# Sketch laid out by head, fewer warm-ups and earlier loads in the prologue of a fused attention and expert kernel

## The chip, the cores and the metric

The kernel runs on one core of one Trainium2 chip. The metric is device microseconds (us) of one execution; lower is better. All runs of one group are made on one chip, with runs of the kernel before between them.

Executions of this program fall into two groups that differ by a little over 1 us. They differ in the mean clock that TensorE was granted over the span. In the four timed groups the kernel before ran 44 times: 25 executions at a granted clock of 0.999 or 1.0 have a median of 500.97 us (499.89 to 501.62), 19 at 0.997 or less have 502.1 us (501.78 to 502.7). I call them full-clock and low-clock executions, and give full-clock medians where an effect is below 1 us. Some kernels have executions at 0.998; I count them as full-clock, since the one that was profiled (b_straight) has its only half-clock stretch of the trace's clock record after 498.15 us, behind the last matmul.

## The reference

```python
def phi(x):                                   # q, k, v: (4, 4, 1088, 32); S1, S2: (8, 32)
    a = np.einsum('rd,bhsd->bhsr', S1, x)
    b = np.einsum('rd,bhsd->bhsr', S2, x)
    return np.einsum('bhsi,bhsj->bhsij', a, b).reshape(*x.shape[:-1], r * r)
q_p, k_p = (phi(q), phi(k))
kv = np.einsum('bhsf,bhsd->bhfd', k_p, v)
z = np.sum(k_p, axis=2)
attn = num / (den + 1e-06)                    # num from kv, den from z
x = attn.transpose(0, 2, 1, 3).reshape(4352, 128)
p = domain_probs / (domain_probs.sum(-1, keepdims=True) + 1e-09)
for e in range(4):                            # w1: (4, 128, 1024), w2: (4, 1024, 128)
    h = np.maximum(x @ w1[e], 0.0)
    out += p[:, e:e + 1] * (h @ w2[e])
```

## The kernel before

The kernel is one long pipeline on TensorE. A prologue prepares the first 128 tokens: the sketch matrices S1 and S2 are converted from float64 bits, the keys of batch 0 are transposed (kT), projected (h), multiplied into features (kp), summed over all tokens (f, then kvz), and the first queries are attended (den, num, xT). After that, expert matmuls of 11 chunks of tokens run without a break, and the attention of later tokens is worked in between. The first and the last chunk (128 tokens) take plain matmuls; the middle ones use a scheme with seven products, for which GpSimd forms sums of the second layer's weights (w2s).

The loads, and the warm-up that raises TensorE's clock while they are under way:

```python
s_raw = cpool.tile([32, 2 * D], I32, name="s_raw")
nc.vector.memset(s_raw[:, :], 0)
for i, (eng, src) in enumerate(((nc.scalar, S1), (nc.sync, S2))):
    eng.dma_start(s_raw[R * i : R * i + R, :], src.bitcast(I32))
...
load_rows(k, 0, "kn")
load_rows(q, 0, "qn", slice(0, P))
...
nc.scalar.activation(idle[:, :], warm[:, 0:1], ACTF.Identity)
vn[0] = load_v(0, (nc.sync, nc.scalar))        # two value loads on the sync queue, two on scalar's
...
for i, t in enumerate((0, (B - 1) * S + G - 4)):
    nc.sync.dma_start(
        ends[:, i, :], bass.AP(domain_probs.tensor, domain_probs.offset + t * E, [[G * E, 32], [1, 4 * E]])
    )
load_rows(q, 0, "qn", slice(P, S))
for e in range(E):
    load_w1(e)
    load_w2(e)
...
for _ in range(14):
    wp = psum(ps_h, "h")
    nc.tensor.matmul(wp[:, :], warm[:, 0:P], warm[:, :], start=True, stop=True)
```

The end of a plain chunk, which is also the end of the program:

```python
if e == E - 1:
    t = (START[m] // S) * S + START[m] % S // 32
    nc.sync.dma_start(
        bass.AP(out.tensor, out.offset + t * DM, [[G * DM, 32], [1, 4 * DM]]), total.pop(m)[:, :]
    )
```

The loop hands out one weight sum after each step with `if i: next(to_sum, None)`.

## Time and profile before

| | value |
|---|---|
| time, first three runs | 500.92, 501.15, 500.92 us |
| span of the profiled execution (full clock) | 499.2 us |
| TensorE busy | 490.8 us, 98% |
| first key matmul / first expert matmul begins | 6.88 / 15.49 us |
| last operation on the result (`end`) begins | 495.75 us |

TensorE is busy for 98% of the span, so only three places are left to win at: the prologue before 15.49 us, the hole before "den" near 25 us, and what follows the last matmul. The third is in the timeline of the last microseconds, first VectorE's and then the sync queue's (columns: start, length, engine, line, operation, output<-input, idle time before it and its releaser):

```profile
core 0 of [0], span 499.2 us
...
495.75 0.35 DVE L657 SCALAR_TENSOR_TENSOR end<-o,ends,end 128x128 f32<-128x128 f32 x1 [0.76 <-PE o L186]
...
496.13 0.58 SPq L662 DMA_DIRECT2D out_dram<-end  x1
```

From the last vector operation to the end of the span there are 499.2 - 495.75 = 3.45 us: the operation, the issue of the store, its data, and its completion.

### The profile page before, as it was taken

The page shows a single profiled execution, that of the slowest core. Times are in us where ns is not written, and L with a number is a line of the kernel's source. Part 1 is how long each engine was busy: PE and PEld are TensorE (multiplying, and loading weights), DVE is VectorE, ACT ScalarE, POOL GpSimd, SP SyncE. Part 2 cuts the span into 40 slices and gives each one's busy share as a digit, 9 for nine tenths or more (in the row PEclk, how much of TensorE's full clock was granted, in tenths as well). Part 3 has the DMA queues.
Part 4 walks back from the last instruction along what each step waited for, and adds up shares of the span by engine and source line. Part 5 has one row for each costly group of instructions (what it writes and reads, how often), then busy time and mean ns, then how long its engine had stood idle before and what let it go on. Part 6 is the DMA issues. An engine that isn't in the chain of part 4 may idle for free.

```text
span 499.2 us, 11045 instructions
## 1 busy us (share of the span) xinstructions
PE 490.8 (98%) x4442; PEld 367.8 (74%) x4442; DVE 326.5 (65%) x749; ACT 250.7 (50%) x491; POOL 229.8 (46%) x264
## 2 busy tenths in 40 slices
PE   8899999999999999999999999999999999999997
PEld 6775788777776657777777777777777777788996
DVE  5858675868667585757657646558656557665643
ACT  4543553545454454544545455445455445556662
POOL 6730333444544263444545344344555355655571
PEclk9999999999999999999999999999999999999999
DMA  7981030021002330031001100021001100110000
GB/s 203 286 293 51 1 91 1 2 85 20 1 2 85 66 91 0 1 85 22 3 1 64 43 1 1 2 85 22 2 1 53 23 1 1 43 23 2 14 3 17
DMA packets 29666, 22.36 MB, mean 45 GB/s; under 512 B 20016, under 2 KB 26800, under 8 KB 29232
## 3 DMA queue, kind: packets, MB, share of 16 engines
q1 hardware_dynamic: 29312, 21.40, 15.3%
q8 instruction: 35, 0.57, 0.5%
q10 hardware_dynamic: 304, 0.26, 0.2%
q14 instruction: 15, 0.12, 0.1%
HBM read 19.35 MB, written 2.31 MB: 43 GB/s over the span
## 4 chain that ended last, share of the span: by engine, by line
PE 96%; DVE 3%; issue 0%; ACT 0%; DVEq 0%; ACTq 0%
PE h L186 48%; PE o L186 39%; PE f L186 5%; PE den L186 2%; PE num L186 1%; PE h L176 1%; DVE qp L420 1%; DVE hid L592 1%; DVE qa L479 0%; DVE qf L469 0%; DVE qb L474 0%; DVE qf L471 0%; DVE end L657 0%; ACT hid L618 0%; ACT fs L348 0%
## 5 line engine op out<-in xcount | busy, mean ns | idle before, releaser
L592 DVE SCALAR_TENSOR_TENSOR hid<-h,hid 128x256 f32<-128x256 f32 (+6 forms) x432 | 203.7, 472 | 149.0 <-ACT hid L618 140.7
L186 PE MATMUL h<-xT,w_sb 128*64 128x512 f32 (+4 forms) x1408 | 298.7, 496 | 1.7 <-DVE xT L454 1.4
L618 ACT ACTIVATE hid<-h 128x512 f32<-128x512 f32 (+3 forms) x288 | 158.3, 550 | 202.4 <-PE h L186 169.9
L186 PE MATMUL o<-hid,w2s 128*64 128x256 f32 (+3 forms) x1152 | 220.9, 355 | 0.0
L186 PEld LDWEIGHTS h<-xT,w_sb 128*64 128x64 f32 x1408 | 149.5, 137 | 52.7 <-issue 4.7
L186 PE MATMUL o<-hid,w_sb 128*64 128x256 f32 (+3 forms) x864 | 185.0, 356 | 0.6 <-DVE end L657 0.6
L186 PEld LDWEIGHTS o<-hid,w2s 128*64 128x64 f32 x1152 | 131.5, 137 | 31.7 <-issue 0.6
L733 POOL TENSOR_TENSOR ev<-yz,sh 64x256 f32<-64x256 f32 (+3 forms) x72 | 48.6, 675 | 159.0 <-ACT sh L736 156.3
L186 PEld LDWEIGHTS o<-hid,w_sb 128*64 128x64 f32 x864 | 101.4, 137 | 21.1 <-issue 1.6
L721 POOL TENSOR_TENSOR yz<-ev 128x512 f32<-128x512 f32 (+3 forms) x36 | 42.3, 1175 | 84.1 <-ACT ev L724 83.9
L733 POOL TENSOR_TENSOR ct<-ev 128x512 f32<-128x512 f32 (+3 forms) x36 | 42.2, 1173 | 2.8
L733 POOL TENSOR_TENSOR ct<-ct,gate 128x512 f32<-128x512 f32 (+3 forms) x27 | 31.9, 1183 | 2.1
L733 POOL TENSOR_TENSOR total<-total,ct 128x512 f32<-128x512 f32 (+3 forms) x27 | 31.8, 1177 | 2.1
L420 DVE TENSOR_TENSOR qp<-qa,qb 64x352 f32<-64x352 f32 (+2 forms) x44 | 31.6, 719 | 1.0
L610 ACT ACTIVATE hid<-h 128x256 f32<-128x256 f32 x24 | 15.3, 655 | 18.7 <-PE h L186 18.2
L723 ACT COPY ev<-o 128x512 f32<-128x512 f32 (+3 forms) x36 | 19.4, 538 | 9.4 <-PE o L186 8.9
L186 PE MATMUL o<-w_sb,hid 128*64 128x128 f32 x256 | 24.0, 273 | 0.0
L186 PEld LDWEIGHTS o<-w_sb,hid 128*64 128x64 f32 x256 | 19.9, 137 | 1.7 <-issue 1.5
L724 ACT COPY ev<-o 128x512 f32<-128x512 f32 (+3 forms) x36 | 19.4, 539 | 3.0
L359 DVE TENSOR_TENSOR kp<-fs 128x256 f32<-128x256 f32 (+1 forms) x24 | 16.1, 677 | 0.0
L736 ACT COPY sh<-yz 64x256 f32<-64x256 f32 (+3 forms) x36 | 13.7, 379 | 1.4 <-POOL yz L721 0.5
L737 ACT COPY sh<-yz 64x256 f32<-64x256 f32 (+3 forms) x36 | 13.7, 380 | 0.9
(93 smaller groups left out, 250.8 us busy)
## 6 DMA issues: line engine op xcount, KB each, us to landing
w_sb<-in_moe_w_dram SPq DMA_DIRECT2D x8, 512.0 KB, 7.7
gate<-gates SPq DMA_DIRECT2D x3, 1024.0 KB, 4.9
kn<-in_k_dram SPq DMA_DIRECT2D x4, 544.0 KB, 4.1
gate<-gates SPq DMA_DIRECT2D x2, 960.0 KB, 5.4
vn<-in_v_dram SPq DMA_DIRECT2D x14, 128.0 KB, 5.0
qn<-in_q_dram SPq DMA_DIRECT2D x3, 544.0 KB, 4.1
gate<-gates SPq DMA_DIRECT2D x1, 896.0 KB
out_dram<-ob SPq DMA_DIRECT2D x12, 64.0 KB, 2.0
```

Source lines behind the costliest of these rows:

```text
L186: nc.tensor.matmul(out(s), weights(s), moving(s), **flags)
L359: eng.tensor_tensor(out=_ap(kps[b], 0, P, 256 * t0 + P * p + 64 * x, [[256, n], [32, 2], [R, 4], [1, R]]), in0=in0, in1=_ap(fss[b], 0, P, ...
L420: nc.vector.tensor_tensor(out=qp[p][64 * x : 64 * x + 64, 0:n], in0=qa[64 * p : 64 * p + 64, 0:n], in1=qb[64 * p : 64 * p + 64, 0:n], op=A ...
L592: nc.vector.scalar_tensor_tensor(out=out, in0=src, scalar=0.0, in1=in1, op0=ALU.max, op1=ALU.subtract)
L610: nc.scalar.activation(turned, src, ACTF.Relu)
L618: nc.scalar.activation(hd[:, n * j : n * j + n], hp[:, 0:n], ACTF.Relu)
L721: add = lambda out, in0, in1, op=ALU.add: nc.gpsimd.tensor_tensor(out=out, in0=in0, in1=in1, op=op)
L723: nc.scalar.copy(_ap(ev, 0, P, 0, [[2 * w, 2], [1, w]]), _ap(a0, 0, P, 0, two))
L724: nc.scalar.copy(_ap(ev, 0, P, w, [[2 * w, 2], [1, w]]), _ap(a1, 0, P, 0, two))
L733: add = lambda out, in0, in1, op=ALU.add: nc.gpsimd.tensor_tensor(out=out, in0=in0, in1=in1, op=op)
L736: nc.scalar.copy(sh[HP:P, 0:w], yz[0:HP, 0, 0:w])
L737: nc.scalar.copy(sh[0:HP, 0:w], yz[HP:P, 1, 0:w])
```

## The change

The intent is a shorter prologue and a smoother start of the second chunk. The sketch matrix sk is laid out by head, so that four copies fill it instead of eight. The loads no longer wait for a memset, and the value loads go ahead of the scalar engine's dummy activation. Three sets of first factors of the queries replace four (12 matmuls instead of 16; the profile counts each as two). Eleven warm-ups replace fourteen. The rectified values of the plain chunks are written straight instead of turned, which needs the two `ends` loads and the store of the plain chunks in another order of tokens. The weight sums are handed out in the second half of the first chunk.

```diff
-    s_raw = cpool.tile([32, 2 * D], I32, name="s_raw")
-    nc.vector.memset(s_raw[:, :], 0)
+    s_raw = cpool.tile([R2, 2 * D], I32, name="s_raw")
...
     load_rows(q, 0, "qn", slice(0, P))
+    vn[0] = load_v(0, (nc.sync, nc.scalar))
...
     nc.scalar.activation(idle[:, :], warm[:, 0:1], ACTF.Identity)
-    vn[0] = load_v(0, (nc.sync, nc.scalar))
...
-            ends[:, i, :], bass.AP(domain_probs.tensor, domain_probs.offset + t * E, [[G * E, 32], [1, 4 * E]])
+            ends[:, i, :], bass.AP(domain_probs.tensor, domain_probs.offset + t * E, [[E, 4], [G * E, 32], [1, E]])
...
-    for _ in range(14):
+    for _ in range(11):
...
     for h in range(H):
-        nc.scalar.copy(
-            _ap(sk, 32 * h, 32, R2 * (h // 2) + 4 * (h % 2), [[H * R2, 2], [R, 2], [1, 4]]),
-            _ap(s_T, 0, 32, 0, [[D, 2], [4, 2], [1, 4]]),
-        )
-        nc.scalar.copy(
-            _ap(sk, 32 * h, 32, H * R + R * h, [[H * R2, 2], [1, R]]), _ap(s_T, 0, 32, R, [[D, 2], [1, R]])
-        )
+        nc.scalar.copy(_ap(sk, 32 * h, 32, R2 * h, [[HP, 2], [1, R2]]), _ap(s_T, 0, 32, 0, [[D, 2], [1, R2]]))
... (GpSimd's copies sp and sr: three sets instead of four)
... (key_project and key_product: the same matmuls and products in the layout by head)
-        fq = [psum(ps_o, "o0"), psum(ps_o, "o1")]
-        for i in range(2):
-            for p in range(2):
-                for j in range(2):
-                    both(fq[i][:, n * p : n * p + n], sr[:, 2 * i + p, j, :], qT[:, 0:n], start=(j == 0), stop=(j == 1))
+        fq = [psum(ps_o, "o0"), psum(ps_o, "o1"), psum(ps_n, "num")]
+        for i in range(3):
+            for j in range(2):
+                both(fq[i][:, 0:n], sr[:, i, j, :], qT[:, 0:n], start=(j == 0), stop=(j == 1))
...
-            src = _ap(hp, 0, P, 0, [[n, 2], [32, n // 32], [1, 32]])
-            turned = _ap(hd, 0, P, 0, [[n, 2], [1, n // 32], [n // 32, 32]])
...
-                nc.scalar.activation(turned, src, ACTF.Relu)
+                nc.scalar.activation(hd[:, 0 : 2 * n], hp[:, 0 : 2 * n], ACTF.Relu)
...
-                        bass.AP(out.tensor, out.offset + t * DM, [[G * DM, 32], [1, 4 * DM]]), total.pop(m)[:, :]
+                        bass.AP(out.tensor, out.offset + t * DM, [[DM, 4], [G * DM, 32], [1, DM]]), total.pop(m)[:, :]
...
-            if i:
+            if i > NQ // 2:
                 next(to_sum, None)
```

More of the change, by code (lines that the diff above doesn't have):

```diff
@@ L154 @@
         load_w2(e)
-    own2 = cpool.tile([P, 2], F32, name="own2")
     sk = cpool.tile([P, P], F32, name="sk")
-    sp = cpool.tile([32, 4, HP], F32, name="sp")
-    sr = cpool.tile([P, 4, 2, P], F32, name="sr")
+    sp = cpool.tile([32, 3, 2, 32], F32, name="sp")
+    sr = cpool.tile([P, 3, 2, P], F32, name="sr")
     sq = cpool.tile([P, P], F32, name="sq")
@@ L163 @@
     nc.gpsimd.memset(sq[:, :], 0.0)
-    nc.gpsimd.memset(own2[:, :], 0.0)
-    for h in range(H):
-        nc.gpsimd.memset(own2[32 * h : 32 * h + 32, h % 2 : h % 2 + 1], 1.0)
     kT = cpool.tile([P, P * NT], F32, name="kT")
@@ L171 @@
     nc.gpsimd.memset(vx[64:P, NT - 1, :, 0:D], 0.0)
-    for _ in range(14):
+    own2 = cpool.tile([P, 2], F32, name="own2")
+    nc.gpsimd.memset(own2[:, :], 0.0)
+    for h in range(H):
+        nc.gpsimd.memset(own2[32 * h : 32 * h + 32, h % 2 : h % 2 + 1], 1.0)
+    for _ in range(11):
         wp = psum(ps_h, "h")
@@ L194, in word @@
     def word(name, t=I32):
-        return cpool.tile([32, 2 * D], t, name=f"s_{name}")
+        return cpool.tile([R2, 2 * D], t, name=f"s_{name}")
     def bits(out, in0, s1, op0, s2=None, op1=ALU.bypass):
@@ L201, in either @@
         nc.vector.tensor_tensor(out=out, in0=a, in1=b, op=ALU.bitwise_or)
-    low = _ap(s_raw, 0, 32, 0, [[2, D]])
-    high = _ap(s_raw, 0, 32, 1, [[2, D]])
+    low = _ap(s_raw, 0, R2, 0, [[2, D]])
+    high = _ap(s_raw, 0, R2, 1, [[2, D]])
     hi, lo = slice(0, D), slice(D, 2 * D)
@@ L207 @@
     s_e, s_f, s_m, s_x, s_n = (word(n) for n in ("e", "f", "m", "x", "n"))
-    s_hl, s_T = word("hl", F32), word("T", F32)
+    s_hl = cpool.tile([32, 2 * D], F32, name="s_hl")
+    s_T = cpool.tile([32, 2 * D], F32, name="s_T")
+    nc.vector.memset(s_hl[:, :], 0.0)
     bits(s_f[:, hi], high, 1, shl, 21, shr)
@@ L222 @@
     either(s_f[:, :], s_e[:, :], s_m[:, :])
-    nc.vector.tensor_tensor(out=s_hl[:, :], in0=s_n[:, :], in1=s_f[:, :].bitcast(F32), op=ALU.mult)
+    nc.vector.tensor_tensor(out=s_hl[0:R2, :], in0=s_n[:, :], in1=s_f[:, :].bitcast(F32), op=ALU.mult)
     nc.vector.transpose(s_T[:, :], s_hl[:, :])
     for h in range(H):
-        nc.scalar.copy(
-            _ap(sk, 32 * h, 32, R2 * (h // 2) + 4 * (h % 2), [[H * R2, 2], [R, 2], [1, 4]]),
-            _ap(s_T, 0, 32, 0, [[D, 2], [4, 2], [1, 4]]),
-        )
-        nc.scalar.copy(
-            _ap(sk, 32 * h, 32, H * R + R * h, [[H * R2, 2], [1, R]]), _ap(s_T, 0, 32, R, [[D, 2], [1, R]])
-        )
-    for i in range(2):
-        for j in range(2):
-            nc.gpsimd.tensor_copy(
-                _ap(sp, 0, 32, HP * (2 * i + j), [[32, 2], [R, 4], [1, R]]),
-                _ap(s_T, 0, 32, D * j, [[4, 2], [1, 4], [0, R]]) if i else _ap(s_T, 0, 32, D * j + R, [[0, 2], [0, 4], [1, R]]),
-            )
-    for h in range(H):
-        for i in range(2):
-            nc.gpsimd.tensor_copy(
-                _ap(sr, 32 * h, 32, P * (4 * i + 2 * (h // 2)) + 32 * (h % 2), [[P, 2], [HP, 2], [1, 32]]),
-                _ap(sp, 0, 32, P * i, [[HP, 2], [32, 2], [1, 32]]),
-            )
+        nc.scalar.copy(_ap(sk, 32 * h, 32, R2 * h, [[HP, 2], [1, R2]]), _ap(s_T, 0, 32, 0, [[D, 2], [1, R2]]))
+    for i in range(3):
+        nc.gpsimd.tensor_copy(
+            _ap(sp, 0, 32, HP * i, [[32, 2], [R, 4], [1, R]]),
+            _ap(s_T, 0, 32, 4 * (i - 1) if i else R, [[D, 2]] + ([[1, 4], [0, R]] if i else [[0, 4], [1, R]])),
+        )
+    for h in range(H):
+        nc.gpsimd.tensor_copy(
+            _ap(sr, 32 * h, 32, 32 * h, [[P, 6], [1, 32]]), _ap(sp, 0, 32, 0, [[32, 6], [1, 32]])
+        )
     mask_lo = [R2 + l % R2 for l in range(32)]
@@ L336, in key_project @@
         if gi == 0:
-            fss[b] = apool.tile([P, 4, NT, R2], F32, tag="fs", name="fs")
+            fss[b] = apool.tile([P, 2, NT, 32], F32, tag="fs", name="fs")
             kps[b] = apool.tile([P, NT, 2, P], F32, tag="kp", name="kp")
@@ L340, in key_project @@
             for i in range(2):
-                both(
-                    kf[:, HP * t : HP * t + HP],
-                    kT[:, P * (t0 + t) : P * (t0 + t + 1)],
-                    sk[:, HP * i : HP * i + HP],
-                    start=(i == 0),
-                    stop=(i == 1),
-                )
+                for _ in range(2):
+                    on_side(
+                        lambda s: _ap(kf, HP * s, HP, 32 * t, [[P, 2], [1, 32]]),
+                        lambda s: kT[:, P * (t0 + t) + HP * s : P * (t0 + t) + HP * s + HP],
+                        lambda s: sk[:, HP * i : HP * i + HP],
+                        start=(i == 0),
+                        stop=(i == 1),
+                    )
         nc.scalar.copy(
-            _ap(fss[b], 0, P, R2 * t0, [[R2, n], [R2 * NT, 4], [1, R2]]),
-            _ap(kf, 0, P, 0, [[HP, n], [R2, 4], [1, R2]]),
+            _ap(fss[b], 0, P, 32 * t0, [[32 * NT, 2], [1, 32 * n]]), _ap(kf, 0, P, 0, [[P, 2], [1, 32 * n]])
         )
     def key_product(b, t0, n, p, x, eng, kf=None):
-        if kf is None:
-            in0 = _ap(fss[b], 0, P, R2 * (NT * p + t0) + R * x, [[R2, n], [4, 2], [1, 4], [0, R]])
-        else:
-            in0 = _ap(kf, 0, P, R2 * p + R * x, [[HP, n], [4, 2], [1, 4], [0, R]])
+        src, off = (kf, P * p) if kf is not None else (fss[b], 32 * (NT * p + t0))
         eng.tensor_tensor(
             out=_ap(kps[b], 0, P, 256 * t0 + P * p + 64 * x, [[256, n], [32, 2], [R, 4], [1, R]]),
-            in0=in0,
-            in1=_ap(fss[b], 0, P, R2 * (NT * (2 + p) + t0), [[R2, n], [R, 2], [0, 4], [1, R]]),
+            in0=_ap(src, 0, P, off + 4 * x, [[32, n], [R2, 2], [1, 4], [0, R]]),
+            in1=_ap(fss[b], 0, P, 32 * (NT * p + t0) + R, [[32, n], [R2, 2], [0, 4], [1, R]]),
             op=ALU.mult,
@@ L521, in start @@
             pass
-        fq = [psum(ps_o, "o0"), psum(ps_o, "o1")]
-        for i in range(2):
-            for p in range(2):
-                for j in range(2):
-                    both(fq[i][:, n * p : n * p + n], sr[:, 2 * i + p, j, :], qT[:, 0:n], start=(j == 0), stop=(j == 1))
+        fq = [psum(ps_o, "o0"), psum(ps_o, "o1"), psum(ps_n, "num")]
+        for i in range(3):
+            for j in range(2):
+                both(fq[i][:, 0:n], sr[:, i, j, :], qT[:, 0:n], start=(j == 0), stop=(j == 1))
         qb = apool.tile([P, QW], F32, tag="qb", name="qb")
-        nc.scalar.copy(qb[:, 0 : 2 * n], fq[0][:, 0 : 2 * n])
+        nc.scalar.copy(qb[:, 0:n], fq[0][:, 0:n])
         for x in range(2):
@@ L543, in start @@
         qp = query_tiles()
-        for p in range(2):
-            nc.vector.tensor_tensor(
-                out=qp[p][:, 0:n], in0=fq[1][:, n * p : n * p + n], in1=qb[:, n * p : n * p + n], op=ALU.mult
-            )
+        for x in range(2):
+            for p in range(2):
+                query_product(qp, p, x, n, fq[1 + x], qb)
         key_divide(b, kv)
@@ L603, in first @@
                 )
-            src = _ap(hp, 0, P, 0, [[n, 2], [32, n // 32], [1, 32]])
-            turned = _ap(hd, 0, P, 0, [[n, 2], [1, n // 32], [n // 32, 32]])
             if m and kq % 2:
-                nc.vector.tensor_scalar(out=turned, in0=src, scalar1=0.0, scalar2=None, op0=ALU.max)
+                nc.vector.tensor_scalar(
+                    out=hd[:, 0 : 2 * n], in0=hp[:, 0 : 2 * n], scalar1=0.0, scalar2=None, op0=ALU.max
+                )
             else:
-                nc.scalar.activation(turned, src, ACTF.Relu)
+                nc.scalar.activation(hd[:, 0 : 2 * n], hp[:, 0 : 2 * n], ACTF.Relu)
             work()
```

## The prediction

> **What bounds the kernel now.** I read the page's busy shares first, then the chain that ended last, then the timeline of the first 30 us and of the last 8 us, and last the order of instructions on each engine in both kernels. The busy shares say that TensorE is the bound, so only time in which TensorE waits, or works on something that the change removes, can be won.
>
> ```profile
> PE 490.8 (98%) x4442; PEld 367.8 (74%) x4442; DVE 326.5 (65%) x749; ACT 250.7 (50%) x491; POOL 229.8 (46%) x264
> ```
>
> The span is 499.2 us, so TensorE is not busy in 8.4 us. A table of busy time by stretch puts 1.25 us of that in the first 12 us, 1.85 us at 12 to 16 us, 0.5 us at 20 to 30, 0.9 us at 30 to 60, and some 3.5 us after the last matmul. From 60 to 480 us it is 0.5 us. "Busy" hides one more loss: warm-up matmuls count as busy. The chain of the first 16 us shows it (start, length, what):
>
> ```profile
> 0.81 0.11 DVE s_raw L118
> 0.92 0.28 DVE warm L135
> 1.25 5.63 PE h L176 x14
> 6.88 2.25 PE h L186 x72
> 9.13 1.75 PE o L186 x32
> 10.88 2.15 PE f L186 x72
> 13.12 0.30 DVE kvz L382
> 13.47 0.46 PE den L186 x4
> 13.96 0.33 DVE dT L442
> ```
>
> Fourteen warm-up matmuls hold TensorE until 6.88; then come key projections, query factors (o), key sums (f), and a chain across VectorE until the first expert matmul at 15.49. Everything before 15.49 is a prologue that shifts the whole rest. What else could have let the keys start earlier is in the timeline (start, length, engine, line, what; the bracket is idle time and its releaser):
>
> ```profile
> 0.95 0.41 SPq L120 DMA_DIRECT2D s_raw<-in_S_dram  x1
> 1.41 0.37 SPq L93 DMA_DIRECT2D kn<-in_k_dram  x1
> ...
> 2.76 0.17 DVE L198 TENSOR_SCALAR s_f<-s_raw 32x32 int32<-32x32 int32 x1 [1.56 <-DMA s_raw<-in_S_dram]
> ...
> 5.25 1.30 DVE L318 STREAM_TRANSPOSE kT<-kn 128x512 f32<-128x512 f32 x2 [0.52 <-DMA kn<-in_k_dram]
> ...
> 5.90 0.20 ACT L235 COPY sk<-s_T 32x16 f32<-32x16 f32 x1
> ```
>
> The first half of kT is done at 5.25 + 0.65 = 5.90, the eighth copy into sk at 6.10. So the inputs of the first key matmul were there at 6.10 and TensorE came at 6.88.
>
> **What the Trainium skill says.** "TensorE: Matmul & The Clock Gate", What's actually happening: the array starts at half clock and is released by some 3.4 us of sustained work, by time and not by number of matmuls, with a free-running window. The trace agrees in kind: the warm-up weight loads are 0.43 us apart from 1.65 to 5.92, then 0.37. So eleven warm-ups should still reach about the release. "DMA: Bandwidth & Descriptors", Anatomy of one DMA: about 2 us of fixed cost, whatever the size. Here the 2 KB sketch is issued at 0.95 and used at 2.76, 1.8 us. It follows that issuing 0.2 us sooner lands 0.2 us sooner. "SBUF — State Buffer", SBUF: two separate sides: a VectorE operation with two SBUF inputs and a GpSimd operation that reads SBUF lock each other out. The trace agrees: two 64x480 products took 2.07 us beside the weight sums and 0.66 us each without them, and a sum went from 0.73 to 1.15 us:
>
> ```profile
> 21.20 2.07 DVE L420 TENSOR_TENSOR qp<-qa,qb 64x480 f32<-64x480 f32 x2
> ...
> 21.61 1.15 POOL L502 TENSOR_TENSOR w2s<-w_sb,w2s 128x256 f32<-128x256 f32 x1
> ...
> 41.67 0.66 DVE L420 TENSOR_TENSOR qp<-qa,qb 64x480 f32<-64x480 f32 x1
> ```
>
> **The change part by part.**
> *Loads without the memset's wait.* The other engines begin at 0.73 to 0.81, the sync queue at 0.95 because it waits for s_raw's memset. Without it the sketch and the keys are issued about 0.2 us sooner: sketch at 2.56, s_T at 4.55 instead of 4.75, kn at about 5.0. The scalar queue's two value loads no longer wait for the dummy activation, so they move by about as much and compete with kn as before. The first half of kT is then done at about 5.65.
> *Four sketch copies instead of eight.* The eight took 4.83 to 6.10, 0.16 us each; four end at 4.63 + 0.64, about 5.3. They are no longer last.
> *Eleven warm-ups.* Warm-up begins at about 1.14 (no memset ahead of it); its eleventh ended 0.96 us before the end of all in the spacing of before (6.88 against 5.92), so it ends near 5.8. TensorE then begins the keys at about 5.8 instead of 6.88: **1.08 us**.
> *Key projection by head.* 36 matmuls of 64 columns before and after, only their output is laid out otherwise: 2.25 us, no change. The same holds for the copy out (128x256, 0.37 us) and the products, in all batches; there they are beside expert matmuls.
> *Three sets of factors.* 16 matmuls become 12, so 1.75 us becomes 1.75 x 12/16 = 1.31: **0.44 us**. On VectorE two 128x128 products of 0.29 us become four of half the partitions, about 0.9 us in all instead of 0.5. They come after the key products, which I put at an end of 10.1 (before 10.83; one copy waits for the values, below). So they end at 11.0, while the key sums run from 9.36 to 11.5: beside TensorE.
> *GpSimd's copies.* Three sp of 0.19 and four sr of 32x192, say 0.37 us (32x128 took 0.28): done at about 6.6, needed at 8.05.
> *Relu without turning.* The turned 128x256 took 0.65 us, the straight one of another chunk 0.385 us. But the first chunk steps every 0.87 us, all of it TensorE (16 matmuls at 0.055), so the 16 x 0.27 us are beside it. In the last chunk likewise: its last 23 matmuls run in 1.41 us with no wait. The result's store has the same 128 rows of 512 B; its tail stays.
> *Weight sums later.* In the program GpSimd's sums now stand behind the gate's product pn, and three of sixteen behind the first gather. But nothing makes them wait for "the second half": GpSimd takes the next instruction as soon as its inputs are there. In the shifted clock they begin at roughly 16 us and run back to back over the four query products, as before. So I give this **0**: the 0.42 us that each product loses to the sums stays, and with it the hole at 25.24 to 26.35, where "den" waits for those products.
>
> Sum: 1.08 + 0.44 = 1.52 us. Key sums, the 2.37 us from kvz to the first expert matmul, and all of the rest follow unchanged; the instruction order of TensorE after the prologue is identical in both kernels. First expert matmul: 15.49 - 1.52 = 13.97. Time: 500.92 - 1.52 = 499.4 us.
>
> **The rivals.**
> *A load takes over.* The loads do not move by 1.5 us, only by 0.2. The last of the four value loads landed at 7.8 (read from the landings in the trace); the copy vx then waits until about 7.6, where the scalar engine would be ready at 7.3. That delays the second key copy to about 8.6 and VectorE's products to 10.1, still 0.8 us ahead of need. w1 of expert 0 landed at 12.5, w2 at 15.5, against needs of 13.97 and 17.66 - 1.52 = 16.1. The slots of the DMA semaphores are dealt anew: the last load of q now follows a wait for a value load (landed 7.26) plus a gate load of 0.65 us, so it and the weights may come 0.4 us later: 15.9 against 16.1. If it is worse than that, TensorE stands 0.2 to 0.5 us at the first second-layer matmul: 499.7 to 499.9.
> *The clock falls or comes late.* If the keys arrive late after eleven warm-ups, or if the window opens later, part of the 72 weight-and-matmul passes runs at half clock: at most 2 us lost, 501. The spacing above speaks against it: only about 0.2 us of work would lie before the release, 0.1 us.
> *Keys do not land earlier.* Bandwidth is shared, so kn could stay at 5.25. TensorE would start at 6.0: gain 0.88 + 0.44 = 1.3, 499.6.
> *The sums do move.* If the products ran without them, the hole before "den" (about 1.1 us) would close: 498.3. Against it: GpSimd's order, which has no wait that would hold them back.
>
> **Range and chances.** The two terms are long durations on a chain that I can follow, and the spread of the runs is 0.2 us. 8 in 10: 498.8 to 500.2, from a gain of 0.7 (loads or clock eat half) to 2.1 (part of the den hole closes too). Two per cent would be 10 us; the whole prologue until 15.49 holds less than that in idle time, and nothing after it changes on TensorE. Faster 0.02, same 0.97, slower 0.01.
>
> **What would show it.** Right: eleven warm-ups ending near 5.8, keys' first matmul within 0.1 us of the later of that and kT; the factor matmuls at 1.31 us; kvz near 11.6, first expert matmul near 14.0; the query products still near 1.0 us each beside sums; a constant lead of 1.5 us from there to the end. Wrong: a wait of TensorE on a load of weights between 14 and 20 us; warm-up spacing still 0.43 us followed by slow key matmuls; sums that start only after 22 us; or a lead that grows or shrinks in the stretch from 20 to 45 us.

## The result, and the profile after

Ratios in this document are the mean time of one kernel's runs over that of the other's of the same rounds, so they are not quite the ratio of the medians quoted beside them.

| | median us | range | runs |
|---|---|---|---|
| before | 501.03 | 500.82 to 502.43 | 6 |
| after | 500.81 | 500.69 to 502.44 | 6 |

The ratio is 0.9994, with a 95% interval of 0.9976 to 1.0011: within 2%, as the chances said, but the predicted gain of 1.5 us is not there, and 500.81 lies above the range of 498.8 to 500.2.

The profiled execution of these six (502.44 us) was a low-clock one. To compare like with like I ran the unchanged kernel again; that profile is a full-clock one with a span of 499.2 us, exactly that of before. Its busy shares:

```profile
PE 489.6 (98%) x4431; PEld 367.0 (74%) x4431; DVE 325.1 (65%) x751; ACT 244.0 (49%) x487; POOL 228.6 (46%) x259
```

TensorE has 1.2 us less work than before (490.8), and yet the span is the same. The chain of the first 16 us (start, length, what) shows where the work left and where waiting came:

```profile
0.74 0.39 SPq L119
1.13 0.06 issue
1.19 4.75 DMA kn<-in_k_dram
5.94 0.02 issue
5.97 0.72 DVE kT L309
6.69 0.14 issue
6.82 2.32 PE h L185 x72
9.14 0.88 PE o L185 x16
10.02 0.44 PE num L185 x8
10.45 2.12 PE f L185 x72
...
12.67 0.30 DVE kvz L371
...
```

The warm-ups are gone from the chain. The keys' load stands in their place: it is issued at 1.19, sooner than the 1.41 of before, and yet kT's transposes begin at 5.97 where they began at 5.25. So the first key matmul comes at 6.82, where the chain of before has it at 6.88 (its timeline, 6.81). After that the chain does what was predicted: the factor matmuls (o and num) take 0.88 + 0.44 = 1.32 us instead of 1.75. The first expert matmul begins at 15.09 instead of 15.49. At the other end of the same trace, first VectorE and then the sync queue:

```profile
core 0 of [0], span 499.2 us
...
495.25 0.35 DVE L642 SCALAR_TENSOR_TENSOR end<-o,ends,end 128x128 f32<-128x128 f32 x1 [0.89 <-PE o L185]
...
495.63 0.60 SPq L647 DMA_DIRECT2D out_dram<-end  x1
```

The last operation comes 0.50 us sooner than before, and from it to the end there are 499.2 - 495.25 = 3.95 us instead of 3.45. The balance of these two traces is then: 0.40 us won in the prologue, 0.10 us more on the way, and 0.50 us lost in the tail.

So two questions are to be answered: why the keys do not land sooner, and why the tail is longer. My theory at this point was that the change itself makes the keys late, since the scalar queue's value loads, issued sooner, share the DMA engines with them, and that the store's new order of dimensions costs the 0.5 us. The rivals were that the keys' landing at 5.25 in the one profile of before was a lucky one, and that a late load of w1 is the bound: in the first profile after, unlike this one, the first expert matmul waits for it.

```profile
15.11 2.12 PE L185 MATMUL h<-xT,w_sb 128*64 128x128 f32 x24 [1.64 <-DMA w_sb<-in_moe_w_dram]
```

### The profile page after: what moved, and what is told of

The parts are those of the page before. It is cut to its first block, busy times and chain, and to the rows that moved or that the text cites. A ratio compares the mean times of both kernels' runs of the same rounds, so it can differ in the third digit from the quotient of the medians.

```text
span 500.6 us, 11017 instructions
## 1 busy us (share of the span) xinstructions
PE 491.1 (98%) x4431; PEld 368.2 (74%) x4431; DVE 324.7 (65%) x751; ACT 243.8 (49%) x487; POOL 228.2 (46%) x259
## 4 chain that ended last, share of the span: by engine, by line
PE 94%; DMA 2%; DVE 2%; SPq 0%; issue 0%; ACT 0%; ACTq 0%
PE h L185 47%; PE o L185 39%; PE f L185 4%; PE den L185 2%; DMA w_sb<-in_moe_w_dram 1%; PE num L185 1%; DMA vn<-in_v_dram 1%; DVE qp L409 1%; DVE hid L578 1%; SPq L147 0%; DVE qa L468 0%; DVE qf L458 0%; DVE qb L463 0%; DVE qf L460 0%; DVE end L642 0%
## 5 line engine op out<-in xcount | busy, mean ns | idle before, releaser
L595 ACT ACTIVATE hid<-h 128x256 f32<-128x256 f32 x24 | 9.2, 383 | 24.8 <-PE h L185 24.3
```

What stands on the lines that cost most here:

```text
L595: nc.scalar.activation(hd[:, 0 : 2 * n], hp[:, 0 : 2 * n], ACTF.Relu)
```

## The experiments

Twelve kernels ran, all correct, in four groups. Unless said otherwise an edit is made to the changed kernel. Full-clock medians of before in the groups are 501.08, 500.84, 500.58 and 501.19 us. The groups ran on four different chips, and the changed kernel itself, apart from the result above, is in the first group only. A comparison of a later group with its 500.70 us therefore crosses chips, and differences of a few tenths are not safe there.

### First group: the changed kernel again, the tail, the value loads, w1 first

**The changed kernel again** (after_again), no edit.

> The changed kernel again, because its profile fell into an execution of 502.44 us in which TensorE ran at half clock from about 15 to 19 us, while its other five executions took 500.69 to 500.89. My theory (loads and store): most executions keep the clock; in the profile of such a one the keys land at about 5.7 (before 5.25), the first key matmul comes at about 6.6, the last byte of expert 0's first weights at about 15.0 and the first expert matmul with it, 0.4 us ahead of before (15.49); the stretch from the last operation on 'end' to the end of the span is about 3.95 us (before 3.45). Front 0.4 us won, tail 0.5 us lost, time within 0.3 us of before. Rival (clock): the changed kernel loses its gain in most executions to TensorE's clock; then a profile at a granted clock of 0.999 or more would show the first expert matmul near 14 and a tail as before, and would be at 499.5.

Measured: four full-clock runs with a median of 500.70 us (500.54 to 501.05), two low-clock ones at 502.2 and 502.37; ratio 0.9994 [0.9976, 1.0011]. The profile is the one shown above. The first result stands.

**The last part undone** (a_turned): rectified values turned again, loads of `ends` and the store as before.

```diff
-            ends[:, i, :], bass.AP(..., [[E, 4], [G * E, 32], [1, E]])
+            ends[:, i, :], bass.AP(..., [[G * E, 32], [1, 4 * E]])
...
-                nc.scalar.activation(hd[:, 0 : 2 * n], hp[:, 0 : 2 * n], ACTF.Relu)
+                nc.scalar.activation(turned, src, ACTF.Relu)        # and VectorE's likewise
...
-                        bass.AP(out.tensor, out.offset + t * DM, [[DM, 4], [G * DM, 32], [1, DM]]), ...
+                        bass.AP(out.tensor, out.offset + t * DM, [[G * DM, 32], [1, 4 * DM]]), ...
```

> The changed kernel with only the last part undone: relu turned again, the gate ends and the end chunks' store in the layout of before. Theory (store's layout): the store whose first dimension is 4 lands through 4 of the DMA engines instead of 16; undone, the tail after the start of the last operation on 'end' goes back from 3.96 to about 3.45 us, and the time is 0.5 us shorter than the changed kernel: about 500.3 against 500.8. Rival (the store costs nothing, the 0.5 us of the profile was chance): tail and time as in the changed kernel, 500.8. Rival (turned relu matters): 16 relus of 0.65 instead of 0.38 us would make it slower, 501 or more.

Measured: full-clock median 500.32 us (four runs, 500.25 to 500.64), 0.38 below the changed kernel; one low-clock run at 501.68; ratio 0.9981 [0.9964, 0.9998]. The end of its trace, VectorE and sync queue:

```profile
core 0 of [0], span 498.6 us
...
495.20 0.35 DVE L642 SCALAR_TENSOR_TENSOR end<-o,ends,end 128x128 f32<-128x128 f32 x1 [0.76 <-PE o L185]
...
495.58 0.58 SPq L647 DMA_DIRECT2D out_dram<-end  x1
```

The last operation begins within 0.05 us of the changed kernel's, and the tail is 498.6 - 495.20 = 3.40 us again. All fourteen profiles divide in this way: 3.39 to 3.45 us with the old store, 3.89 to 3.98 us with the new one. The turned rectification takes 0.65 us a time instead of 0.38, nearly all of it beside TensorE: from the first expert matmul to the last operation there are 480.34 us here, 480.16 in the changed kernel. So the last part costs its 0.5 us in the tail and gives back 0.2 us at most. How the store moves is seen in the DMA view of 495 to 500 us, here of the kernel before (GB/s in 40 slices, then packets):

```profile
GB/s 0 0 0 0 0 0 0 0 0 0 0 0 0 0 0 0 0 0 12 221 254 37 0 0 0 0 0 0 0 0 0 0 0 0 0 0 0 0 0 0
DMA packets 144, 0.07 MB, mean 13 GB/s; under 512 B 16, under 2 KB 144, under 8 KB 144
```

and here of the changed kernel:

```profile
GB/s 0 0 0 0 0 0 0 0 0 0 0 0 0 0 4 49 49 86 90 86 86 74 0 0 0 0 0 0 0 0 0 0 0 0 0 0 0 0 0 0
DMA packets 132, 0.07 MB, mean 13 GB/s; under 512 B 4, under 2 KB 132, under 8 KB 132
```

Both move 128 packets of 512 B. The packets under 512 B are the completion writes, one for each DMA engine that took part: 16 before, 4 after. The data took 0.35 us on 16 engines and 0.91 us on 4 (first to last packet of the store in the two traces). The Trainium skill says so in "DMA: Bandwidth & Descriptors", Why a DMA increments its semaphore by 16 and not by 1: the number of engines is the largest one, up to 16, that divides the slowest dimension (of size above 1) of both access patterns. The new pattern has a slowest dimension of 4. The trace agrees with the count; the page has no time for a store of this size on four engines.

**The value loads behind the dummy activation again** (a_vn_back).

```diff
-    vn[0] = load_v(0, (nc.sync, nc.scalar))
...
     nc.scalar.activation(idle[:, :], warm[:, 0:1], ACTF.Identity)
+    vn[0] = load_v(0, (nc.sync, nc.scalar))
```

> The changed kernel with only the values' load moved back behind the dummy activation. Theory (the scalar queue's value loads take the keys' bandwidth): the keys land at 5.0 to 5.2 instead of 5.7, the first key matmul comes at about 6.0 instead of 6.6, and VectorE's last step of the prologue, xT, 0.5 us sooner; but the first expert matmul still waits for expert 0's first weights near 15, so the time stays within 0.2 us of the changed kernel (500.8). Rival (keys are late for another reason, such as the ring or the memory): keys at 5.7 again. Rival (no gate by the weights): 500.3.

Measured: kT's transposes begin at 5.69, not between 5.0 and 5.2. Full-clock median 500.41 us (five runs, 500.19 to 500.81), one low-clock run at 502.04, which is the profiled one; ratio 0.9984 [0.9967, 1.0]. The theory, in the form that the new place of the value loads makes the keys late, is not borne out; but the edit was a weak test of it, since it moved the scalar queue's value loads only from 1.36 to 1.43 us. The time is 0.29 us below that of the changed kernel, which fits a landing that is 0.28 us sooner in the profiles; but landings between 5.63 and 5.97 occur in kernels that issue all this alike, so I draw nothing from it.

**w1 of expert 0 ahead of the rest of q** (a_w1_first).

```diff
+    load_w1(0)
     load_rows(q, 0, "qn", slice(P, S))
     for e in range(E):
-        load_w1(e)
+        if e:
+            load_w1(e)
         load_w2(e)
```

> The changed kernel with expert 0's first weights issued ahead of the rest of the queries. Theory (weights gate the first expert matmul): they land 1.3 us or more sooner, at 13.7 or before, so the first expert matmul follows xT at about 14.8 instead of 15.1, and the time is 0.3 us shorter, 500.5; the rest of the queries then lands by 15, and its transpose comes some 0.3 us later without holding TensorE. Rival (the weights' wait is only a coincidence of the profiled execution): 500.8. Rival (query transposes become the gate): 501.

Measured: full-clock median 500.76 us (three runs), against 500.70 for the changed kernel; three more in low clock at 501.96 to 502.35; ratio 0.9999 [0.9981, 1.0018]. The wait for w1 was seen in one of the two profiles of the changed kernel (0.28 us longer than the usual 1.36 us for xT), and later in those of a_sums_held and a_memset (0.10 and 0.16 us). Taking away its chance of being late won nothing that the time shows. The rival of w1 falls as the main cause.

### Second group: before once more, the last part alone, the keys alone, the sums held

**The kernel before once more** (before_again), one look.

> The kernel before, unchanged, for a second profile on the chip of these runs. Theory (the change itself makes the keys late, although they are issued 0.2 us sooner): the keys land at 5.2 to 5.3 again, against 5.6 to 6.0 in five profiles with the change's early issue. Rival (the landing of the keys differs from execution to execution or chip to chip): 5.6 or later here too, and then the lateness is no effect of the change. Tail from the last operation on 'end' to the end of the span 3.45 us in both.

Measured: 500.27 us at a clock of 1.0, a single run whose state is unknown. VectorE's and then TensorE's lines for the start of the keys:

```profile
5.79 1.30 DVE L318 STREAM_TRANSPOSE kT<-kn 128x512 f32<-128x512 f32 x2 [0.83 <-DMA kn<-in_k_dram]
...
6.64 2.32 PE L186 MATMUL h<-sk,kT 128*64 128x64 f32 x72 [0.50 <-POOL sr L246]
```

The same kernel, with the memset and the later issue, now has its keys at 5.79 instead of 5.25, and a wait of 0.50 us of TensorE after its fourteen warm-ups, which this time took 4.89 us instead of 5.63. So the two numbers on which my largest term rested, the landing at 5.25 and the end of the warm-ups at 6.88, both move by some 0.5 to 0.7 us from one execution to the next. The rival (a lucky landing) is enough to explain the lateness. The theory that the change makes the keys late isn't needed, but isn't excluded either: with the value loads on two queues, no profile with the sooner issue has a landing before 5.63, and two of the five with the memset have one (5.25 and 5.33).

The profile names GpSimd's sr as what ended the wait of 0.50 us, yet the keys fit better. In eleven of the fourteen profiles the first key matmul begins 0.85 or 0.86 us after kT's transposes, this one among them (5.79 and 6.64). The exceptions are before and b_straight, where the warm-ups held TensorE longer, and b_warm11 (0.91 us).

**The last part alone, on the kernel before** (b_straight): the three edits that a_turned undoes, with everything else as before.

> The kernel before with only the last part of the change: relu without turning, gate ends and end chunks' store with a first dimension of 4. Theory (this store costs 0.5 us on the path): tail 3.95 us instead of 3.45, time about 501.4 in executions at full clock, where the kernel before has 500.9. Rival (the shorter relus of 0.38 instead of 0.65 us give something back): 501.0 or less.

Measured: four full-clock runs, two of them at 0.998, with a median of 501.48 us (500.83 to 501.98), 0.64 above before in the same group; two low-clock ones at 502.52 and 502.71; ratio 1.001 [0.9991, 1.0028]. The times scatter too much to settle 0.5 us alone. The trace does: from the start of the last operation to the end there are 3.89 us, and the store's data took 0.91 us with four completion writes. The tail comes from this part without any other.

**All value loads on the sync queue** (a_kn_alone), behind the keys.

```diff
-    vn[0] = load_v(0, (nc.sync, nc.scalar))
+    vn[0] = load_v(0, (nc.sync, nc.sync))
```

> The changed kernel with all value loads issued by the sync queue, behind the keys, so that no other queue has bytes under way while the keys come. Theory (the scalar queue's value loads take turns with the keys on every engine): the keys land at 5.0 or before instead of 5.6 to 6.0, the first key matmul comes at about 5.9, 0.7 us sooner; the values land later, 8 us or more, and may hold up the copies vx and the key sums for a part of that; the first expert matmul waits for expert 0's first weights (15.0) and moves little; time 500.4 to 500.8. Rival (the keys are late on their own, by receipt or memory): 5.6 again and no gain at all.

Measured, the same two lines:

```profile
4.98 1.30 DVE L309 STREAM_TRANSPOSE kT<-kn 128x512 f32<-128x512 f32 x2 [0.44 <-DMA kn<-in_k_dram]
...
5.84 2.32 PE L185 MATMUL h<-sk,kT 128*64 128x64 f32 x72 [0.79 <-DVE kT L309]
```

The keys are there at 4.98 and the first key matmul begins at 5.84, the two numbers of the prediction (5.0 and 5.8). The first expert matmul begins at 14.04, where 13.97 was predicted. So the two value loads of the scalar queue are what kept the keys late in the changed kernel: they are on the way at the same time, on the same DMA engines. In best2, which has the same edit, they are there at 5.01. On the kernel before it was not run. The Trainium skill describes it in "DMA: Bandwidth & Descriptors", Queues, rings and completion order: each DMA engine goes round between the queues that have work for it, packet by packet. One queue alone brought the keys 0.7 to 1.0 us sooner than two queues at once did. The full-clock median is 500.26 us (four runs, 500.01 to 500.34), only 0.44 below the changed kernel; the two low-clock runs, 501.36 and 501.44, are 0.8 to 1.1 below those of the changed kernel (502.2 to 502.44). Profile against profile in low clock the lead stays: 1.07 us at the first expert matmul (14.04 against 15.11), 1.01 us at the last operation. Why full-clock runs keep less I cannot say, since the only profile of this kernel is a low-clock one. A part of it may be the chip, and 15.09 is late for the changed kernel: with the values on two queues, its variants begin that matmul between 14.70 and 15.11.

**The weight sums truly held back** (a_sums_held): GpSimd takes a tiny copy that needs the second pair of query products, before the sums.

```diff
+    hold = cpool.tile([P, 1], F32, name="hold")
...
+        if b == 0 and c == P:
+            nc.gpsimd.tensor_copy(hold[:, :], qp[1][:, 0:1])
...
-            if i > NQ // 2:
+            if i > 11:
                 next(to_sum, None)
```

> The changed kernel with the weight sums really held back: a one-column GpSimd copy that reads the fourth query product of the first full unit stands before them, so that they cannot start before it. Theory (in the change nothing holds the sums; they run beside the four query products, each of which loses 0.3 to 0.4 us, and TensorE waits for the last before 'den'): the four products take 0.65 us each instead of about 1.0, the wait of TensorE before 'den' shrinks from about 1.1 us to nothing or near it, time 0.7 to 1.1 us shorter than the changed kernel, 499.7 to 500.1. Rival (the products are not what 'den' waits for, or the sums come too late for chunk 1): no gain or a loss.

Measured: the only two full-clock runs are 499.17 and 499.24 us, 1.5 below the changed kernel (up to 0.24 of it can be the chip, by the medians of before); four low-clock ones lie between 500.53 and 501.19, where the changed kernel's are between 502.2 and 502.44. Ratio 0.9977 [0.9959, 0.9996]. VectorE's products in the changed kernel, with a sum on GpSimd beside them, and TensorE's first "den":

```profile
20.79 2.18 DVE L409 TENSOR_TENSOR qp<-qa,qb 64x480 f32<-64x480 f32 x2
...
21.32 1.14 POOL L491 TENSOR_TENSOR w2s<-w_sb 128x256 f32<-128x256 f32 x1
...
23.78 2.10 DVE L409 TENSOR_TENSOR qp<-qa,qb 64x480 f32<-64x480 f32 x2
...
24.83 1.72 PE L185 MATMUL den<-qp,kvz 128*64 128x480 f32 x3 [0.41 <-DVE qp L409]
```

and with the sums held (GpSimd's copy, which waits for the products, and the first sum follow, then "den" without a wait):

```profile
20.60 1.31 DVE L410 TENSOR_TENSOR qp<-qa,qb 64x480 f32<-64x480 f32 x2
...
22.71 1.34 DVE L410 TENSOR_TENSOR qp<-qa,qb 64x480 f32<-64x480 f32 x2
...
24.11 0.18 POOL L475 COPY hold<-qp 128x1 f32<-128x1 f32 x1 [7.36 <-DVE qp L410]
24.25 0.72 POOL L494 TENSOR_TENSOR w2s<-w_sb 128x256 f32<-128x256 f32 x1
...
24.02 1.10 PE L186 MATMUL den<-qp,kvz 128*64 128x480 f32 x4
```

Each pair of products is 0.8 us shorter, and in this trace's chain "den" follows the expert matmul before it at once, at 24.22, where the changed kernel's chain runs through the products and reaches the "den" that needs the last of them only at 25.93. This is the largest single gain, and the changed kernel's own edit (`i > NQ // 2`) does not get it.

### Third group: eleven warm-ups alone, the clock, and a version with all that helped

**Eleven warm-ups in the kernel before** (b_warm11).

```diff
-    for _ in range(14):
+    for _ in range(11):
```

> The kernel before with eleven warm-up matmuls instead of fourteen, nothing else. My prediction gave 1.08 us to the shorter warm-up with sooner keys. Theory now (in most executions the keys land near 5.7, so that the first key matmul can come at 6.6 at the earliest, and fourteen warm-ups end between 6.1 and 7.1 by the moment of the clock's release): the first key matmul comes at 6.5 to 6.8, with TensorE idle before it; gain 0 to 0.4 us, time at full clock 500.5 to 501.0. Rival (the prediction's: warm-ups are the bound): first key matmul near 6.0 to 6.2 and 0.7 to 0.9 us faster.

Measured: kT at 5.33, and TensorE's line for the keys:

```profile
6.24 2.32 PE L186 MATMUL h<-sk,kT 128*64 128x64 f32 x72 [0.97 <-ACT sk L235]
```

With the keys early, the eighth sketch copy is the last to come, as the prediction read from the profile of before. Full-clock median 500.38 us (five runs; a low-clock one took 501.89), against 500.58 of before in the same group; ratio 0.9991 [0.9977, 1.0005]. The warm-ups alone were worth 0.2 us here.

**TensorE kept busy in the hole before the first expert matmul** (a_keepwarm): five dummy matmuls after num, while VectorE works on den.

```diff
-        for _ in attend(b, 0, n, qp):
+        final = attend(b, 0, n, qp)
+        next(final)
+        wp = psum(ps_h, "h")
+        for _ in range(5):
+            nc.tensor.matmul(wp[:, :], warm[:, 0:P], warm[:, :], start=True, stop=True)
+        for _ in final:
             pass
```

> The changed kernel with five dummy matmuls of 512 columns in the hole of about 1.4 us that TensorE has between the first 'num' and the first expert matmul. Theory (the clock falls in part of the executions because of that hole after a prologue with other holes; these are the executions 1.4 to 1.7 us longer at a granted clock of 0.995 to 0.997): no execution at 0.997 or below any more, all within 500.5 to 501.0; the first expert matmul is not later. Rival (the fall has another cause, such as the holes before it or the chip's power): a third to a half of the executions stay at 502. Rival (the dummies delay the first expert matmul): all about 0.3 us longer.

The reason for this run is the table of stretches in the low-clock profile of the changed kernel (columns as in its header; PEclk is the granted clock):

```profile
core 0: us, PE busy (x) PEld busy (x) DVE busy (x) ACT busy (x) POOL busy (x), PEclk, DMA share, GB/s
...
14.00:16.00 2.00, 0.89 (x16) 0.92 (x18) 1.79 (x9) 0.20 (x1) 0.00 (x0) 0.97 1.09 364
16.00:18.00 2.00, 2.00 (x16) 1.50 (x14) 0.27 (x2) 0.95 (x3) 1.57 (x3) 0.50 1.13 348
18.00:20.00 2.00, 2.00 (x23) 1.50 (x21) 1.09 (x3) 0.00 (x0) 1.82 (x4) 0.67 1.15 329
```

The clock falls to half for 3.4 us soon after the hole in which TensorE waits for xT, and 16 matmuls fit where 31 fit at full clock in the other profile of the same kernel. With the hole filled, from TensorE's timeline:

```profile
13.28 1.25 PE L539 MATMUL h<-warm 128*128 128x512 bf16 x4
14.70 1.53 PE L185 MATMUL h<-xT,w_sb 128*64 128x128 f32 x24 [0.17 <-DVE xT L443]
```

Measured: six of six at 0.999 or above, median 500.76 us (500.64 to 501.17); ratio 0.9995 [0.9984, 1.0007]. No gain or loss at full clock is seen (500.70, on another chip), and no low-clock execution. The next kernel has the same edit and gave six of six as well; without it, 31 of 47 timed executions of the changed kernel and its variants were full-clock, and 25 of 44 of before. At such odds twelve in a row would be chance 7 times in a thousand (0.66 to the twelfth). But the chip of this group had few low-clock executions in any case: before and b_warm11 had 14 full-clock ones of 17 on it, and at these odds the twelve would be chance one time in ten. The count alone doesn't show the cause.

The traces say more. Their clock record shows the first release to full clock between 3.88 and 6.88 us (in before_again 4.71, which fits its warm-ups: their spacing shrinks from 0.43 us after 4.64), and in the three low-clock profiles a fall exactly 10.24 us after it, for 3.41 us. Counted in stretches of 3.41 us from the release, here for a_vn_back, where the clock fell, and for a_turned, where it didn't (columns as above):

```profile
11.40:14.81 3.41, 1.59 (x41) 1.21 (x37) 2.53 (x11) 0.00 (x0) 1.20 (x6) 1.00 1.06 359
14.81:18.23 3.42, 3.42 (x28) 2.86 (x30) 1.32 (x6) 1.15 (x3) 1.86 (x4) 0.50 1.10 341
...
11.28:14.70 3.42, 1.76 (x46) 1.38 (x41) 2.23 (x10) 0.00 (x0) 1.18 (x6) 1.00 1.07 363
14.70:18.11 3.41, 3.25 (x48) 2.73 (x50) 2.33 (x10) 1.59 (x3) 1.64 (x3) 1.00 1.10 344
```

TensorE was idle for 3.41 - 1.59 = 1.82 us of the stretch before the fall, and for 1.66 us where none followed. The other two that fell had 1.82 and 1.97 us; none of the eleven that didn't fall had more than 1.78 us in any stretch up to 20 us. With the hole filled, the stretch that holds it has 0.56 us here and 0.69 us in best2. So in these profiles the clock fell where the hole and the waits before it added up to 1.82 us or more within one stretch; the moment of the release, which differs between executions, decides how much of them one stretch holds. In the kernel before, which has the same hole (1.36 us of waiting for xT at 15.49) and the same two groups of times, I did not fill it, and none of its low-clock executions was profiled.

**All that helped, in one kernel** (best2): a_turned, a_kn_alone, a_w1_first, a_keepwarm and a_sums_held together, and the first copy of the values moved behind all three key copies.

> The changed kernel with all that helped: end chunks' store and relu as before, values behind the keys on the sync queue, the three key copies ahead of the value copies, expert 0's first weights ahead of the rest of the queries, five dummy matmuls in the hole, weight sums held back behind the fourth query product. Theory (the parts add): against the changed kernel -0.5 for the store, -0.7 to -1.0 for the keys, -1.5 for the sums: 497.8 to 498.5 in all executions, none at a low clock. Rival (they overlap, or a load of weights becomes the gate at the sooner start): 498.8 to 499.5, with a wait of TensorE on a load between 13 and 18 us.

Measured: 497.89 us median, six runs between 497.87 and 498.26, all full-clock. In the same group before had a full-clock median of 500.58, 2.69 above, and the ratio over all its runs is 0.9939 [0.9927, 0.9951]. This beats both kernels, though by less than 2%. The estimate from the parts, at full clock, was 500.70 - 0.38 (tail) - 1.5 (sums) - 0.44 to 1.05 (keys), so 497.8 to 498.4, and the run falls in it; as the 500.70 comes from another chip, a part of this agreement can be luck. From the chain of 0 to 32 us:

```profile
5.87 2.32 PE h L188 x72
...
14.08 1.53 PE h L188 x24
...
22.97 0.44 PE h L188 x8
23.40 0.92 PE den L188 x4
```

The first expert matmul comes at 14.08, and "den" follows the first layer without a wait.

### Fourth group: the early issue alone

**The memset put back** (a_memset), ahead of the loads, in the changed kernel.

```diff
     s_raw = cpool.tile([R2, 2 * D], I32, name="s_raw")
+    nc.vector.memset(s_raw[:, :], 0)
```

> The changed kernel with the sketch's memset back in front of its loads, so that sketch and keys are issued at 0.95 and 1.41 us again. Theory (what decides the landing of the keys is the values' traffic beside them, which varies from execution to execution; 0.2 us of issue are less than that): keys at 5.2 to 5.8 as in the four profiles of kernels with the memset (5.25, 5.79, 5.69, 5.33), time at full clock within 0.2 us of the changed kernel, 500.5 to 500.9. Rival (the prediction's: the sooner issue is worth 0.2 us): 0.2 us or more longer, 500.9 to 501.1. Rival (the sooner issue even harms): 0.2 us or more shorter.

Measured: kT at 5.71, no later than without the memset (5.76 and 5.97). Full-clock median 500.99 us (four runs, 500.93 to 501.07); two low-clock ones at 502.38 and 502.65; ratio 0.9995 [0.9978, 1.0012]. That is 0.29 above the changed kernel's 500.70, but on another chip, whose kernel before was also 0.11 slower. So in time the sooner issue is worth between nothing and 0.2 us, and it stays open which. The landings agree over all profiles with the values on two queues. From the issue of the keys to kT's transposes there are 3.84 to 4.37 us in the five with the memset, and 4.43 to 4.78 us in the seven without: the keys went out 0.2 us sooner and were on the way about 0.4 us longer. Why they were is not shown.

## Why the prediction was right or wrong

**Where kn lands: wrong, and the cause of the miss.** The step that failed is "kn at about 5.0", from which followed "TensorE then begins the keys at about 5.8 instead of 6.88: 1.08 us". I took the landing of one profile (5.25) as a fixed number and shifted it by the 0.2 us of the sooner issue. The runs put this in its place: with the value loads on two queues, kT began between 5.25 and 5.79 in four profiles with the memset in the kernel before or its variants, and between 5.63 and 5.97 in seven with the sooner issue. The sooner issue brought no sooner landing. In the changed kernel the keys are held by DMA engines that also carry the scalar queue's values: without these, the same issue lands them 0.7 to 1.0 us sooner. I had named this rival ("Bandwidth is shared, so kn could stay at 5.25") and given it too mild an outcome, since I let the keys stay at the luckiest landing. a_kn_alone, which takes the values off the other queue, shows nearly the predicted numbers, 4.98 and 5.84. The prediction's rule "issuing 0.2 us sooner lands 0.2 us sooner" also leaned on a 2 KB load and on a section of the skill ("DMA: Bandwidth & Descriptors", Anatomy of one DMA) that describes DMAs issued by GpSimd. These loads are issued on the sync and scalar queues, and 544 KB beside other loads did not follow the rule.

**The end of the warm-ups: a size that I took from one execution.** Fourteen warm-ups took 5.63, 4.89 and 5.84 us in three profiles of before and b_straight, and eleven took 3.86 to 4.88 us. In before_again they ended early enough that TensorE waited 0.50 us for other inputs. So the 1.08 us were measured from an execution with slow warm-ups and early keys; with the keys of before_again, the same three warm-ups would have been worth almost nothing. b_warm11 measured 0.2 us for them. The pair of traces above shows 0.06 us for the whole term; over all profiles with the values on two queues, TensorE begins the keys at 6.49 to 6.82 us with the change and at 6.64 to 7.01 with fourteen warm-ups, about 0.2 us apart in the mean.

**The 0.44 us of three factor sets: right.** The matmuls took 1.32 us instead of 1.75. **The chain from kvz on: right.** In after_again it takes 15.09 - 12.67 = 2.42 us where 2.37 was predicted, and a_kn_alone, whose keys come when predicted, starts its first expert matmul within 0.07 us of the 13.97.

**"Its tail stays": wrong, by 0.5 us.** The prediction said that the store has "the same 128 rows of 512 B", which is true, and concluded that it costs the same. What sets the time is over how many DMA engines the rows are spread, and the new outermost dimension of 4 confines them to four (0.91 us of data instead of 0.35). a_turned and b_straight show this from both sides. The skill has the rule, and I had not looked it up for this line of the diff. This alone ate the whole 0.4 us that the prologue won.

**The weight sums at 0: right, and more was behind it than I thought.** They began at 16.94 (at 16.93 in before_again, with the old order), and the products stayed at 2.18 and 2.10 us a pair; nothing made GpSimd wait. The rival (the hole before "den", about 1.1 us, would close) named the right place: held by a real dependency, the kernel took 499.2 us, which is 1.3 to 1.5 below the changed one.

**w1 as the gate: partly right.** w1 of expert 0 landed at 14.97 in the first profile after and held TensorE for a moment (whether because the semaphores' slots are dealt anew, no run shows); in the second it didn't. It isn't worth 0.3 us.

**The rectification at 0: right** within 0.2 us, by a_turned. **The clock:** the fear was for the warm-ups. Where the release came after the start of the keys (6.83 and 6.88 us in a_memset and a_w1_first), their matmuls took 2.42 and 2.48 us instead of 2.32, so that cost is 0.1 to 0.2 us, as small as said. What the clock does cost, 1.1 us between the groups' medians of before, comes later: in the profiles of the changed kernel and its variants after the hole before the first expert matmul.

**The sum**, then, was 1.52 and at full clock came out near nothing: 0.44 as predicted, 0.1 to 0.2 in place of 1.08, and -0.5 in place of 0. Still open are why the landing of the keys varies by 0.7 us between profiles, what exactly the sooner issue is worth, and why a_kn_alone keeps less than half of its lead at full clock.

## What to carry to other kernels

A landing time in one profile is a sample: before a term of a sum rests on it, look at what shares the DMA engines with that load, and take it from two or three executions. Look at the outermost dimension of every access pattern that a change touches, above all in the last store, which nothing hides. And an instruction moved later in the program is delayed only if something makes its engine wait; a tiny copy with a real dependency did what the place in the loop did not.

## What the Trainium skill lacked or had wrong

- "DMA: Bandwidth & Descriptors" has the rule for the number of engines right, but no time for a small transfer on few of them: 64 KB in 128 rows of 512 B took 0.35 us of data on 16 engines and 0.91 us on 4, and the end of the program moved by 0.5 us.
- The same page says that loads of several queues interleave, but not what that does to the load needed first: 544 KB of keys were in use at 4.98 and 5.01 us with the values behind them on one queue, and at 5.63 to 5.97 with half of the values on a second one.
- "TensorE: Matmul & The Clock Gate", HAM oscillation — how this bites in real kernels, warns of idle gaps above some 3.4 us. Here a single hole of 1.4 to 1.6 us was enough together with a shorter wait before it: the three profiles in which the clock fell had 1.82 to 1.97 us of idle time, in sum, in the 3.41 us before the fall, and no stretch of the eleven others had more than 1.78 us in the first 20 us.
- The same page, What's actually happening, gives ±500 ns for the moment at which the clock is released. Here the traces have it between 3.88 and 6.88 us, with warm-ups that begin at 1.19 to 1.26 us in all of them, and fourteen warm-ups took 4.89 to 5.84 us.
